# Cross-covariance attention and highway layer: stage 2 of a batch interleaved with the Gram sums of the next

## The chip, the cores and the metric

The kernel runs on one core of a Trainium2 chip. The metric is device time in microseconds, from the first to the last instruction of the core with what lies around it; lower is better. The time before is 414.52 us, the median of 3 runs (414.21 to 415.14).

TensorE (PE in the rows) multiplies 128x128 stationary tiles with moving tiles into PSUM; VectorE (DVE), ScalarE (ACT) and GpSimd (POOL) work on 128 partitions; SyncE (SP) only issues transfers here. Each engine runs its own instructions in order and waits on semaphores for the others.

## What is computed

There are four batches of 6336 rows and 256 channels. `tau` is 1.

```python
B, N, C = (4, 6336, 256)
qn = q / (np.linalg.norm(q, axis=1, keepdims=True) + 1e-06)
kn = k / (np.linalg.norm(k, axis=1, keepdims=True) + 1e-06)
s = kn.transpose(0, 2, 1) @ qn / tau
a = softmax of s over its last axis
x = (v @ a).reshape(B * N, C)
H = np.maximum(x @ w_h, 0.0)
T = 1.0 / (1.0 + np.exp(-(x @ w_t + b_t)))
out = T * H + (1.0 - T) * x
```

Inputs and output are fp32. The kernel loads q, k, v and the weights as fp16, and the transfer does the conversion. Read are 78 MB in all, written 26 MB.

## The kernel before

A sub-tile is 128 rows of one batch with all 256 channels; a batch has 49 full sub-tiles and a last one of 64 rows. Sub-tile s holds rows s·128 to s·128 + 127, one row a partition, so a partition reads runs of one row, 1 KB in HBM.

**Loads.** `_load_group` (L398) issues from POOL: one transfer for 16 sub-tiles (L401), and one for each sub-tile of the last group (L408). `load_qk` and `load_v` place these calls in the program. All q and k of a batch fit in their buffers (four each), v has three.

**Stage 1** (L120 to L149) runs over the 50 sub-tiles of a batch. For each half c of the channels it adds three products to `sg`: k by q (256 columns), k by k and q by q (128 columns each; their diagonals are the squared norms). That is 512 columns a half and six matmuls a sub-tile.

**The chain** (L151 to L248) makes of `sg` the matrix `mr`. ACT copies `sg` to `ssb`; DVE sums the diagonals (L162); ACT takes roots (L172, with a table load); DVE inverts them and spreads those of q into `dcat` (L178); TensorE broadcasts it (`cqb`); DVE scales (L193); ACT takes the exponential (L202, with a table load); DVE sums the rows, inverts and writes the softmax into the first 256 columns of `mr` (L210). TensorE transposes it and multiplies it by both weight matrices (`ahat`), which fills columns 256 to 767. So v has to be multiplied by `mr` only once.

**Stage 2** (L254 to L395) runs over pairs of sub-tiles, 24 full pairs and the last sub-tiles apart. `emit_transpose` transposes a pair of v with four matmuls by the identity into fp32 PSUM (`vtps`, L284), and DVE (L296) or ACT (L301), in turn, copies it to `vtsb` as fp16. It is called two pairs ahead. The pair is then multiplied by `mr`: columns 0 to 511 into `p3a` (x and H, one tile for each sub-tile, three buffers), columns 512 to 767 into `p3b`, to which a matmul with the identity adds the bias (L343). ACT makes `uu`, 1 − T (L354), and `hh`, the relu (L366). DVE makes `dd` = hh − x for each sub-tile (L370, 256 columns), POOL makes `pp` = uu·dd for the pair (L378, 512 columns), and DVE makes `o` = hh − pp (L382). SP stores eight sub-tiles at a time (L418).

**What sets the order.** The program is written batch after batch, stage 1, chain, stage 2. The framework's scheduler reorders it within its buffers, so that on TensorE some of the Gram sums of a batch stand between parts of stage 2 of the one before, and on DVE the steps of several pairs stand between each other. On each engine the result is one fixed row of instructions. A load on POOL takes the next of eight completion slots and waits until the load that had it last has landed.

## Time and profile before

| | before |
|---|---|
| median of the runs | 414.52 us |
| span of the profiled execution | 412.4 us |
| PE busy | 297.5 us (72%) |
| DVE busy | 208.9 us (51%) |
| ACT busy | 183.3 us (44%) |
| POOL busy | 189.2 us (46%) |
| DMA queue of POOL, share of 16 engines | 70.3% |
| DMA queue of SP, share of 16 engines | 20.6% |
| granted TensorE clock, mean | 0.950 of full speed |

The runs' time stands 2.1 us above the span of the profiled execution, which counts from the first to the last instruction. Busy time is counted per engine and overlaps between engines; a matmul's recorded length includes its way through the array, so that matmuls in a row start closer together than they last. The busy shares are means over stages with different limits, so the rows further below are mostly from single stretches.

### The profile page before, as it was taken

The numbers are of one execution on the slowest core, as the hardware profiler recorded it, in microseconds if no ns is written. First come the engines' busy times: TensorE is split into PE (matmuls) and PEld (weight loads), VectorE is DVE, ScalarE is ACT, GpSimd is POOL, SyncE is SP. The second block draws the span as 40 slices with busy tenths as digits, with TensorE's granted clock in tenths as the row PEclk, the third lists the DMA queues.
The fourth block names the chain that finished last, engine by engine and source line by source line (L and its number), as shares of the span: only waits on it lengthen the run. The fifth ranks groups of instructions, "written<-read, shape, count | busy, mean of one in ns | idle before, by whom it ended". The sixth has DMA issues, their size and how long they took to land.

```text
span 412.4 us, 6770 instructions
## 1 busy us (share of the span) xinstructions
PE 297.5 (72%) x2637; PEld 212.1 (51%) x2637; DVE 208.9 (51%) x426; ACT 183.3 (44%) x407; POOL 189.2 (46%) x173
## 2 busy tenths in 40 slices
PE   0186839809877899968777999777778938776770
PEld 0176737506544698544445986444447815444440
DVE  0000103707876704497767232887766144786663
ACT  1000126605655306756555055566552166655561
POOL 9212322634646634555548441557366002754453
PEclk9999969957999999999999999999999968999996
DMA  7999999999962999999439999494329700433333
GB/s 95 198 199 197 198 198 199 197 233 188 195 193 70 217 245 198 197 222 241 124 103 173 238 205 198 94 209 138 109 67 215 163 0 0 113 102 103 103 102 121
DMA packets 103456, 65.57 MB, mean 159 GB/s; under 512 B 1537, under 2 KB 103425, under 8 KB 103425
## 3 DMA queue, kind: packets, MB, share of 16 engines
q0 software_dynamic: 77568, 39.20, 70.3%
q1 hardware_dynamic: 25856, 25.95, 20.6%
q8 instruction: 20, 0.33, 0.3%
q14 instruction: 12, 0.09, 0.1%
HBM read 78.38 MB, written 25.95 MB: 253 GB/s over the span
## 4 chain that ended last, share of the span: by engine, by line
PE 24%; DMA 24%; DVE 23%; POOL 17%; issue 7%; ACT 4%; POOLq 0%; DVEq 0%; ACTq 0%
POOL pp L378 15%; DVE o L382 14%; DMA k<-in_k_dram 14%; DVE dd L370 7%; PE p3a L336 7%; DMA v<-in_v_dram 6%; PE sg L129 5%; DMA q<-in_q_dram 4%; PE p3b L329 3%; PE sg L136 2%; PE sg L143 2%; PE vtps L284 2%; ACT hh L366 2%; PE p3b L343 1%; DVE vtsb L296 1%
## 5 line engine op out<-in xcount | busy, mean ns | idle before, releaser
L378 POOL TENSOR_TENSOR pp<-uu,dd 128x512 f32<-128x512 f32 (+1 forms) x104 | 131.4, 1273 | 144.0 <-DVE dd L370 64.8
L336 PE MATMUL p3a<-mr,vtsb 128*128 128x512 f16 (+1 forms) x400 | 134.7, 385 | 33.6 <-DVE dd L370 33.5
L382 DVE TENSOR_TENSOR o<-hh,pp 128x512 f32<-128x512 f32 (+1 forms) x104 | 94.4, 923 | 52.3 <-POOL pp L378 52.3
L366 ACT ACTIVATE hh<-p3a 128x256 f32<-128x256 f32 x200 | 76.1, 386 | 87.1 <-PE p3a L336 57.5
L129 PE MATMUL sg<-q,k 128*128 128x256 f16 (+1 forms) x400 | 94.7, 281 | 25.0 <-DMA k<-in_k_dram 24.1
L329 PE MATMUL p3b<-mr,vtsb 128*128 128x256 f16 (+1 forms) x400 | 100.3, 276 | 0.6 <-ACT uu L354 0.5
L370 DVE TENSOR_TENSOR dd<-hh,p3a 128x256 f32<-128x256 f32 x200 | 75.4, 413 | 29.2 <-ACT hh L366 29.0
L136 PE MATMUL sg<-k 128*128 128x128 f16 (+1 forms) x400 | 89.8, 225 | 0.0
L143 PE MATMUL sg<-q 128*128 128x128 f16 (+1 forms) x400 | 89.7, 224 | 0.0
L296 DVE CAST vtsb<-vtps 128x512 f16<-128x512 f32 (+1 forms) x52 | 34.5, 664 | 98.4 <-PE vtps L284 98.1
L284 PE MATMUL vtps<-ident,v 128*128 128x128 f16 (+1 forms) x400 | 41.1, 222 | 34.9 <-DVE vtsb L296 22.7
L336 PEld LDWEIGHTS <-vtsb 128*128 128x128 f16 (+1 forms) x400 | 39.3, 99 | 42.4 <-issue 18.9
L329 PEld LDWEIGHTS <-vtsb 128*128 128x128 f16 (+1 forms) x400 | 39.3, 99 | 42.2 <-issue 26.7
L354 ACT ACTIVATE uu<-p3b 128x512 f32<-128x512 f32 (+1 forms) x104 | 59.8, 579 | 0.1
L284 PEld LDWEIGHTS <-v 128*128 128x128 f16 (+1 forms) x400 | 30.8, 99 | 54.2 <-issue 32.6
L129 PEld LDWEIGHTS <-k 128*128 128x128 f16 (+1 forms) x400 | 40.2, 100 | 30.5 <-DMA k<-in_k_dram 29.9
L343 PE MATMUL p3b<-btb,ident 128*128 128x256 f16 x200 | 55.2, 276 | 0.0
L143 PEld LDWEIGHTS <-q 128*128 128x128 f16 (+1 forms) x400 | 40.2, 101 | 6.9 <-issue 1.1
L301 ACT CAST vtsb<-vtps 128x512 f16<-128x512 f32 (+1 forms) x52 | 29.3, 563 | 29.2 <-PE vtps L284 29.2
L153 ACT COPY ssb<-sg 128x512 f32<-128x512 f32 x8 | 4.3, 589 | 84.7 <-PE sg L143 84.7
L136 PEld LDWEIGHTS <-k 128*128 128x128 f16 (+1 forms) x400 | 40.2, 101 | 1.7 <-issue 1.4
L401 POOL DMA_DIRECT2D k<-in_k_dram x12 | 14.1, 1176 | 27.9 <-PE sg L143 23.5
(44 smaller groups left out, 123.2 us busy)
## 6 DMA issues: line engine op xcount, KB each, us to landing
out_dram<-o SPq DMA_DIRECT2D x24, 1024.0 KB, 5.4
q<-in_q_dram POOLq DMA_DIRECT2D x12, 1024.0 KB, 19.6
k<-in_k_dram POOLq DMA_DIRECT2D x12, 1024.0 KB, 17.4
...
```

Of the source, the lines that this page charges most:

```text
L129: nc.tensor.matmul(sg[c][:, 0:C], kt_[0:nr, si, bass.ts(c, P)], qt[0:nr, si, :], start=first, stop=False,)
L136: nc.tensor.matmul(sg[c][:, C : C + P], kt_[0:nr, si, bass.ts(c, P)], kt_[0:nr, si, bass.ts(c, P)], start=False, stop=False,)
L143: nc.tensor.matmul(sg[c][:, C + P : C + 2 * P], qt[0:nr, si, bass.ts(c, P)], qt[0:nr, si, bass.ts(c, P)], start=False, stop=last,)
L284: nc.tensor.matmul(vtps[:, u, c, 0:nr], vt_in[0:nr, si + u, bass.ts(c, P)], ident[0:nr, 0:nr], start=(pcnt == 0), stop=(pcnt == 2 * pn - 1),)
L329: nc.tensor.matmul(p3b[0:nr, u, :], vt_sb[:, u, kt, 0:nr], mr[:, kt, 2 * C : 3 * C], start=(kt == 0 and u == 0), stop=False,)
L336: nc.tensor.matmul(pa[0:nr, :], vt_sb[:, u, kt, 0:nr], mr[:, kt, 0 : 2 * C], start=(kt == 0), stop=(kt == 1),)
L343: nc.tensor.matmul(p3b[0:nr, u, :], ident[:, 0:nr], btb, start=False, stop=(u == pn - 1),)
L354: nc.scalar.activation(out=uu[0:nr0, 0:pn, :], in_=p3b[0:nr0, 0:pn, :], func=Act.Sigmoid, scale=-1.0,)
L366: nc.scalar.activation(out=hh[0:nr, u, :], in_=p3a[u][0:nr, C : 2 * C], func=Act.Relu,)
L370: nc.vector.tensor_tensor(out=dd[0:nr, u, :], in0=hh[0:nr, u, :], in1=p3a[u][0:nr, 0:C], op=AluOp.subtract,)
L378: nc.gpsimd.tensor_tensor(out=pp[0:nr0, 0:pn, :], in0=uu[0:nr0, 0:pn, :], in1=dd[0:nr0, 0:pn, :], op=AluOp.mult,)
L382: nc.vector.tensor_tensor(out=ostg[0:nr0, si : si + pn, :], in0=hh[0:nr0, 0:pn, :], in1=pp[0:nr0, 0:pn, :], op=AluOp.subtract,)
```

## The change

The body of the kernel is written anew. What is computed stays; the two small constants of the reference are now added as well (1e-6 to the norms, 1e-9 to the sums).

**Layout.** Row p·49 + s of the first 6272 rows of a batch goes to partition p, so a chunk of 8 or 9 sub-tiles is one run of 8 or 9 KB per partition in HBM, for loads and stores. The last 64 rows of all four batches are loaded together, once for each of q, k and v (`tails`). q and k have nine buffers of a chunk each, v seven, the output three.

**Order.** The framework's scheduler is off (`manual_schedule`); what is written is what each engine runs. Stage 1 of batch 0 stands alone. Then in every pair of stage 2 TensorE gets: the pair's products, the transposes of the pair after next, and in pairs 0 to 17 a share of the 50 sub-tiles of the next batch's Gram sums. The five steps of the next batch's chain follow in pairs 18 to 22, one a pair. `issue_loads` places loads as soon as the buffer's last use stands earlier in the program.

**Steps.** Transposes are fp16 transposes into fp16 PSUM, all copied by DVE. `xh` takes the place of `p3a`, for a pair at once; the bias is one matmul of 512 columns a pair. `hh` and `dd` are one instruction a pair. The product is written over `dd`. `o` of a pair is written after the products of the next. The chain reads `sg` in PSUM, uses one scratch tile for the four diagonals, gets the row sums from the exponential, and multiplies in fp32 for the broadcast. PSUM: `sg` 2 banks, `xh` 2 × 2, `t` 1, `vt` 1.

```diff
-    GS = 16
-    OGS = 8
+NCH = [8, 8, 8, 8, 8, 9]
+QK_BUFS = 9
+V_BUFS = 7
+S1_SLOTS = 18
+LOOK = 2
...
+    ctx.enter_context(tc.manual_schedule())
...
+    def main_rows(src2d):
+        return src2d[0 : P * S, :].rearrange("(p s) c -> p s c", p=P)
+
+    def load_chunk(src, b, j, tag, bufs, store):
+        t = stream.tile([P, CM, C], f16, tag=tag, bufs=bufs, name=f"{tag}{b}_{j}")
+        n = NCH[j]
+        nc.gpsimd.dma_start(
+            out=t[:, 0:n, :], in_=main_rows(src[b])[:, c_start[j] : c_start[j] + n, :]
+        )
...
+    load_chunk(q, 0, 0, "q", QK_BUFS, q_t)
+    load_chunk(k, 0, 0, "k", QK_BUFS, k_t)
...
+        for j in range(NJ):
+            seq.append(("v", b, j))
+            if b + 1 < B:
+                seq.append(("q", b + 1, j))
+                seq.append(("k", b + 1, j))
...
+    def issue_loads():
+        while ptr[0] < len(seq):
+            kind, b, j = seq[ptr[0]]
+            bufs = V_BUFS if kind == "v" else QK_BUFS
+            prev = b * NJ + j - bufs
+            if prev >= 0:
+                at = done_use.get((kind, prev))
+                if at is None or at >= clock[0]:
+                    return
...
-                nc.vector.tensor_copy(
-                    out=vt_sb[:, 0:pn, :, 0 : nrows[0]],
-                    in_=vtps[:, 0:pn, :, 0 : nrows[0]],
-                )
-            else:
-                nc.scalar.copy(
...
+    def transposes(b, i):
+        ps = psum.tile([P, 2, 2, P], f16, tag="vt", bufs=1, name=f"vtps{b}_{i}")
+        for u, (src, nr) in enumerate(pair(b, i)):
+            for c in range(2):
+                nc.tensor.transpose(ps[:, u, c, 0:nr], src[:, bass.ts(c, P)], ident[0:nr, 0:nr])
...
+            nc.vector.tensor_copy(
+                out=vt[:, u0 : u0 + nu, :, 0:nr], in_=ps[:, u0 : u0 + nu, :, 0:nr]
+            )
...
+        xh = psum.tile([P, 2, 2 * C], f32, tag="xh", bufs=2, name=f"xh{b}_{i}")
+        tt = psum.tile([P, 2, C], f32, tag="t", bufs=1, name=f"t{b}_{i}")
...
+            nc.vector.tensor_tensor(
+                out=dd[0:nr, us, :],
+                in0=hh[0:nr, us, :],
+                in1=xh[0:nr, us, 0:C],
+                op=AluOp.subtract,
+            )
...
+            nc.gpsimd.tensor_tensor(
+                out=dd[0:nr, us, :], in0=uu[0:nr, us, :], in1=dd[0:nr, us, :], op=AluOp.mult
+            )
...
+    issue_loads()
+    for step in chain(0):
+        step()
+    for i in range(LOOK):
+        transposes(0, i)
...
+        for i in range(npair):
+            clock[0] += 1
+            xh, tt = main(b, i)
+            if pending is not None:
+                pending()
+            pending = elementwise(b, i, xh, tt)
+            n = i + LOOK
+            if n < npair:
+                transposes(b, n)
+            elif nxt:
+                transposes(b + 1, n - npair)
+            issue_loads()
+            if nxt:
+                want = min(S + 1, -(-(S + 1) * (i + 1) // S1_SLOTS))
+                while s1 < want:
+                    stage1(b + 1, s1)
+                    s1 += 1
+                if s1 == S + 1:
+                    if steps is None:
+                        steps = chain(b + 1)
+                    elif steps:
+                        steps.pop(0)()
```

Three places show how the rows of instructions change.

POOL, ahead of its first product of stage 2 in batch 0, before (the number in a tile's name is its place in the batch, `_460` and the like tell tiles apart; DMASW0 to DMASW7 are the completion slots):

```order
L401 DMA q_1_464<-in_q_dram 128x16x256 [waits DMASW0_49,PE_49]
L401 DMA k_1_465<-in_k_dram 128x16x256 [waits DMASW1_49]
L401 DMA q_2_468<-in_q_dram 128x16x256 [waits DMASW2_49,PE_49]
L401 DMA k_2_469<-in_k_dram 128x16x256 [waits DMASW3_49]
L408 DMA q_3_472<-in_q_dram 128x256 [waits DMASW4_49,PE_49]
L408 DMA q_3_472<-in_q_dram 64x256 [waits DMASW5_49]
L408 DMA k_3_473<-in_k_dram 128x256 [waits DMASW6_49]
L408 DMA k_3_473<-in_k_dram 64x256 [waits DMASW7_49]
L401 DMA v_0_478<-in_v_dram 128x16x256 [waits DMASW0_49]
L401 DMA v_1_480<-in_v_dram 128x16x256 [waits DMASW1_49]
L378 TENSOR_TENSOR pp_0_0_525<-uu_0_0_517,dd_0_0_520 128x512 [waits DVE_49,Activation_49]
```

Now the loads ahead of the first product end with the first chunks of v for batch 1 and of q and k for batch 2:

```order
L74 DMA v_4_442<-in_v_dram 128x2048 [waits DMASW7_49]
L74 DMA q_4_444<-in_q_dram 128x2048 [waits DMASW0_49,PE_49]
L74 DMA k_4_446<-in_k_dram 128x2048 [waits DMASW1_49]
L74 DMA v_5_448<-in_v_dram 128x2304 [waits DMASW2_49]
L74 DMA q_5_450<-in_q_dram 128x2304 [waits DMASW3_49,PE_49]
L74 DMA k_5_452<-in_k_dram 128x2304 [waits DMASW4_49]
L74 DMA v_0_454<-in_v_dram 128x2048 [waits DMASW5_49]
L74 DMA q_0_456<-in_q_dram 128x2048 [waits DMASW6_49,PE_49]
L74 DMA k_0_458<-in_k_dram 128x2048 [waits DMASW7_49]
L367 TENSOR_TENSOR dd_0_532<-uu_0_531,dd_0_532 128x512 [waits DVE_49,Activation_49]
L367 TENSOR_TENSOR dd_1_578<-uu_1_577,dd_1_578 128x512 [waits DVE_49,Activation_49]
```

What moved: where two chunks of v of the running batch and the rest of the next batch's q and k were last ahead of the product, more loads of a later use now are.

DVE in stage 2 of batch 1, before: the `dd` of two or three pairs, then their `o`.

```order
L370 TENSOR_TENSOR dd_0_8_1819<-hh_0_8_1818,p3a_8_1804 128x256
L370 TENSOR_TENSOR dd_0_8_1819<-hh_0_8_1818,p3a_9_1810 128x256
L370 TENSOR_TENSOR dd_0_10_1850<-hh_0_10_1849,p3a_10_1835 128x256
L296 CAST vtsb_1_0_1866<-vtps_1_0_1861 128x512
L370 TENSOR_TENSOR dd_0_10_1850<-hh_0_10_1849,p3a_11_1841 128x256
L370 TENSOR_TENSOR dd_0_12_1884<-hh_0_12_1883,p3a_12_1869 128x256
L370 TENSOR_TENSOR dd_0_12_1884<-hh_0_12_1883,p3a_13_1875 128x256
L382 TENSOR_TENSOR o_0_1657<-hh_0_8_1818,pp_0_8_1824 128x512
L382 TENSOR_TENSOR o_0_1657<-hh_0_10_1849,pp_0_10_1855 128x512
L382 TENSOR_TENSOR o_0_1657<-hh_0_12_1883,pp_0_12_1889 128x512
```

Now three instructions a pair, always in the same order (batch 0, pairs 2 and 3):

```order
L359 TENSOR_TENSOR dd_2_622<-hh_2_620,xh_2_608 128x512
L306 COPY vtsb_4_632<-vtps_4_627 128x512
L384 TENSOR_TENSOR o_0_574<-hh_2_620,dd_2_622 128x512
L359 TENSOR_TENSOR dd_3_672<-hh_3_670,xh_3_658 128x512
L306 COPY vtsb_5_682<-vtps_5_677 128x512
L384 TENSOR_TENSOR o_0_574<-hh_3_670,dd_3_672 128x512
```

The copy of the pair after next now stands between a pair's `dd` and its `o`, and `o` ahead of the next `dd`.

DVE at the chain, before (batch 1's chain, behind the last `o` of batch 0):

```order
L162 SCALAR_TENSOR_TENSOR junk_1591,nrm_1592<-ssb_1587,ident_70 128x128 x4
L296 CAST vtsb_0_4_1677<-vtps_0_4_1672 128x512
L174 RECIPROCAL inv_1599<-nrt_1597 128x4
L178 TENSOR_SCALAR dcat_1601<-ident_70,inv_1599 128x128 x2
L193 SCALAR_TENSOR_TENSOR t_1608<-ssb_1587,inv_1599,cqbs_1606 128x256 x2
L204 TENSOR_REDUCE rs_1613<-araw_1611 128x2
L208 RECIPROCAL rinv_1615<-rs_1613 128x2
L210 TENSOR_SCALAR mr_1590<-araw_1611,rinv_1615 128x256 x2
```

Now (batch 1's chain, in pairs 18 to 20 of batch 0):

```order
L306 COPY vtsb_20_1344<-vtps_20_1339 128x512
L181 SCALAR_TENSOR_TENSOR junk_1352,nrm_1353<-sg_544,ident_76 128x128 x4
L193 TENSOR_SCALAR inv_1360<-nrm_1358 128x4
L196 RECIPROCAL inv_1360<-inv_1360 128x4
L200 TENSOR_SCALAR dcat_1363<-ident_76,inv_1360 128x128 x2
L384 TENSOR_TENSOR o_4_1292<-hh_18_1332,dd_18_1334 128x512
L359 TENSOR_TENSOR dd_19_1380<-hh_19_1378,xh_19_1366 128x512
L306 COPY vtsb_21_1390<-vtps_21_1385 128x512
L384 TENSOR_TENSOR o_4_1292<-hh_19_1378,dd_19_1380 128x512
L359 TENSOR_TENSOR dd_20_1411<-hh_20_1409,xh_20_1396 128x512
L306 COPY vtsb_22_1421<-vtps_22_1416 128x512
L220 TENSOR_TENSOR t_1423<-sg_544,cqbs_1394 128x256 x2
```

The steps of the chain now stand between the copy of a pair and an `o`.

## Rows read from the trace of the kernel before

**Rows 1.** The head of the page.
```profile
span 412.4 us, 6770 instructions
```

**Rows 2.** Chain of waits in time order, first products of batches (start, length, what).
```profile
165.55 0.43 PE p3a L336 x2
...
252.51 0.43 PE p3a L336 x2
```

**Rows 3.** Busy time by stretch: length, PE, PEld, DVE, ACT, POOL, clock, DMA, GB/s.
```profile
168.00:223.00 55.00, 42.07 (x308) 26.36 (x306) 41.05 (x77) 34.11 (x82) 33.06 (x28) 1.00 0.90 173
```

**Rows 4.** Timeline of POOL: start, length, what, [idle before <- releaser].
```profile
3.74 1.21 POOL L401 DMA_DIRECT2D q<-in_q_dram  x1
...
67.78 1.15 POOL L401 DMA_DIRECT2D v<-in_v_dram  x1 [3.93 <-DMA k<-in_k_dram]
73.14 1.27 POOL L378 TENSOR_TENSOR pp<-uu,dd 128x512 f32<-128x512 f32 x1 [4.21 <-ACT uu L354]
```

**Rows 5.** DMA: 20 to 60 us, then by queue 137 to 153 us.
```profile
DMA packets 15584, 7.92 MB, mean 198 GB/s; under 512 B 176, under 2 KB 15582, under 8 KB 15582
...
q0 software_dynamic: 4473, 2.27, 104.0%
q1 hardware_dynamic: 1431, 1.40, 30.4%
```

**Rows 6.** Timeline of DVE in stage 2 of batch 2.
```profile
272.65 0.74 DVE L370 TENSOR_TENSOR dd<-hh,p3a 128x256 f32<-128x256 f32 x2
...
274.83 0.69 DVE L382 TENSOR_TENSOR o<-hh,pp 128x512 f32<-128x512 f32 x1 [0.84 <-POOL pp L378]
275.44 1.07 DVE L370 TENSOR_TENSOR dd<-hh,p3a 128x256 f32<-128x256 f32 x3
```

**Rows 7.** Timeline of POOL at the same place.
```profile
273.53 1.26 POOL L378 TENSOR_TENSOR pp<-uu,dd 128x512 f32<-128x512 f32 x1 [2.57 <-DVE dd L370]
276.26 1.26 POOL L378 TENSOR_TENSOR pp<-uu,dd 128x512 f32<-128x512 f32 x1 [1.47 <-DVE dd L370]
```

**Rows 8.** Timeline of PE in stage 1 of batch 1 and stage 2 of batch 2.
```profile
139.76 0.27 PE L129 MATMUL sg<-q,k 128*128 128x256 f16 x1
...
140.20 0.27 PE L129 MATMUL sg<-q,k 128*128 128x256 f16 x1
...
267.71 0.39 PE L284 MATMUL vtps<-ident,v 128*128 128x128 f16 x4
267.93 0.27 PE L329 MATMUL p3b<-mr,vtsb 128*128 128x256 f16 x1
...
269.45 0.39 PE L284 MATMUL vtps<-ident,v 128*128 128x128 f16 x4
```

**Rows 9.** Groups of instructions by line (xcount | busy us, mean ns | idle before).
```profile
L284 PE MATMUL vtps<-ident,v 128*128 128x128 f16 (+1 forms) x400 | 41.1, 222 | 34.9 <-DVE vtsb L296 22.7 <-DMA v<-in_v_dram 10.5 <-ACT vtsb L301 1.4
...
L172 ACT ACT_TABLE_LOAD x4 | 5.1, 1283 | 0.1
...
L162 DVE SCALAR_TENSOR_TENSOR junk<-ssb,ident 128x128 f32<-128x128 f32 x16 | 3.7, 285 | 0.0
L193 DVE SCALAR_TENSOR_TENSOR t<-ssb,inv,cqbs 128x256 f32<-128x256 f32 x8 | 3.5, 481 | 2.6 <-ACT cqbs L189 2.6
...
L210 DVE TENSOR_SCALAR mr<-araw,rinv 128x256 f16<-128x256 f32 x8 | 2.5, 351 | 0.1
...
L178 DVE TENSOR_SCALAR dcat<-ident,inv 128x128 f16<-128x128 f32 x8 | 1.9, 284 | 0.1
...
L174 DVE RECIPROCAL inv<-nrt 128x4 f32<-128x4 f32 x4 | 0.7, 178 | 10.5 <-ACT nrt L172 10.5
```

**Rows 10.** One line's or tile's instructions: ns min/median/max, first/last start; landings of stores.
```profile
L408 POOL DMA_DIRECT2D k<-in_k_dram x8: 528/561/590, 13.8 to 243.8; - x8
...
L378 POOL TENSOR_TENSOR pp<-uu,dd x104: 716/1267/1865, 73.1 to 407.2; 128x512 f32<-128x512 f32 x96, 128x256 f32<-128x256 f32 x4, 64x256 f32<-64x256 f32 x4
...
DMA to landing us min/median/max: 4.4/5.4/10.8
```

More of the change, by code (lines that the diff above doesn't have):

```diff
@@ new lines @@
+    ctx.enter_context(tc.manual_schedule())
+    q_t, k_t, v_t = {}, {}, {}
+    tails = {}
+    def main_rows(src2d):
[6 more added lines that the diff above has]
+        )
+        store[(b, j)] = t
@@ L74 @@
+    ones = const.tile([P, P], f32, tag="ones")
+    nc.vector.memset(ones, 1.0)
+    for j in range(1, 3):
+        load_chunk(q, 0, j, "q", QK_BUFS, q_t)
+        load_chunk(k, 0, j, "k", QK_BUFS, k_t)
+    wht = const.tile([P, 2, 2 * C], f16, tag="wht")
+    nc.gpsimd.dma_start(out=wht[:, :, 0:C], in_=moe_w_h.rearrange("(kt jl) m -> jl kt m", kt=2))
     nc.gpsimd.dma_start(
@@ new lines @@
+    for i in range(S + 1):
+        stage1(0, i)
+        clock[0] += 0.001
+    clock[0] += 1
[4 more added lines that the diff above has]
+        transposes(0, i)
+    pending = None
+    for b in range(B):
+        nxt = b + 1 < B
+        s1 = 0
+        steps = None
+        for i in range(npair):
+            clock[0] += 1
+            xh, tt = main(b, i)
[18 more added lines that the diff above has]
+                        steps.pop(0)()
+        while nxt and steps:
+            steps.pop(0)()
```

597 lines of the change are left out of this document (254 added, 343 removed).

## Prediction

> **What bounds the kernel now.** I read the stage windows first, then the chain of waits, then the timelines of POOL, DVE and PE. The chain of waits gives the rhythm: the first product of a batch on TensorE starts at 165.55 us in batch 1 and at 252.51 in batch 2 [rows 2], so a batch costs 87 us. Inside it no engine is full: in a stretch of stage 2, 55 us long, PE is busy 42, DVE 41, POOL 33 at a granted clock of 1.00 [rows 3]. What is late there is a loop through two engines. DVE subtracts (`dd`), POOL multiplies (`pp`), DVE subtracts again (`o`): `dd` starts at 272.65, `pp` at 273.53, `o` at 274.83, the next `dd` at 275.44, its `pp` at 276.26 [rows 6, 7]. Where the three follow each other like this, a pair of sub-tiles costs 2.7 to 2.8 us. TensorE needs less: at full clock a pair of stage 2 takes 269.45 − 267.71 = 1.74 us, and half a sub-tile of the Gram sums 0.22 us (two starts of L129, 0.44 us apart, hold both halves), so 0.44 us for a whole one [rows 8]. Per batch that is 25 × 1.74 + 50 × 0.44 = 65.5 us of PE.
>
> The front is bound by transfers. While only loads run, 198 GB/s of fp16 land, 396 GB/s as read in fp32 [rows 5]. POOL issues all loads, in program order, with eight completion slots: each issue waits until the load eight back has landed. At 67.78 POOL still waits for such a landing, and its first product of stage 2 is at 73.14 [rows 4].
>
> **1. The front.** All loads up to the last prefetch now stand on POOL ahead of the first product: 21 chunks of 8 or 9 sub-tiles stand there beyond batch 0's q and k, the tails and the weights. The last of them, `k_0_458`, waits for slot 7, that is for `v_4_442`. Read until then: q and k of batch 0 with 12.85 MB, weights and bias 0.79, three tails 0.79, five chunks of v 5.24, eight chunks of q and k of batch 1 8.39, together 28.05 MB; at 396 GB/s 70.8 us. The same count for before (24.0 MB by 67.78) leaves 7.2 us of start-up. q now goes first instead of at 3.74 [rows 4], so this is between 3.5 and 7.2; I take 4.8. Issuing the last load takes 0.56 us, the row of a load with one run per partition [rows 10]. The first product can start at 70.8 + 4.8 + 0.56 = 76 us. Batch 0's q and k land by 41 us (14.2 MB), and its Gram sums and some 10 us of softmax end by about 52: they hide under this, and DVE's first `o`, behind which TensorE soon waits too, stands until POOL comes.
>
> Runs per partition in HBM grow from 1 KB to 8 or 9 KB. No row shows such a load. For the slow end I take the store rate worked out in part 4 (311 GB/s; a rival of its own below), for the fast end as much the other way (480 GB/s: a front of 64 us); 396, the only load row, is the value.
> The Trainium skill, page "DMA: Bandwidth & Descriptors", section "Why small descriptors are slow (HBM only)", gives about 3 cycles of overhead per packet; estimated from it, with 32 cycles for 1 KB, the front would be 6 us shorter and the whole 370 us.
>
> **2. The pace of stage 2.** The new order on DVE is fixed: `dd` of a pair, the copy of a transposed pair, `o`, then the next `dd`. `o` waits for POOL's product, the product waits for `dd`, and the next `dd` stands behind `o`. The loop found above is thus closed for every pair, where before DVE often ran two pairs of `dd` ahead. Its length: `dd` on 512 columns in one piece 0.68 us (one piece of `o` with the same columns is 0.69 [rows 6]), hop to POOL 0.14 (0.74 us of two `dd` from 272.65, product at 273.53), product 1.26, hop 0.04, and 0.61 from the start of `o` to the next `dd` [rows 6, 7]: 2.73 us. The copy lies within the product and costs nothing while it ends before it (some 0.7 us, as `o` with the same columns, against 1.26); so its faster fp16 source, and that ACT has lost half of these copies, gain nothing here. Should POOL become shorter, the copy would be next.
>
> TensorE takes 1.74 us for stage 2 plus 50 sub-tiles over 18 pairs, 2.78 × 0.44 = 1.22: 2.96 us in pairs 0 to 17, and 1.74 in pairs 18 to 24. Against the loop this is 18 × 0.23 = 4.1 us too long, but PE enters each batch ahead, by what two buffers of `xh` allow; between 0 and 4.1, I take 1. Bias and product columns are the same as before.
>
> Pair 24 is in two pieces: 0.61 + 0.75 + 0.14 + 2 × 0.72 + 0.04 = 3.0 us (0.75 as two `dd` of 256 columns, shortest product 0.716 us [rows 10]).
>
> **3. The softmax chain between pairs 18 and 22.** Its steps are now in DVE's line. The norms: four reductions into one scratch tile, each waiting for the one before, 4 × 0.35 (0.285 and 0.07 for the hop); square root and hops 0.4; two short operations and two of 0.28, with hops 0.93 [rows 9]. Of these 2.7 us, 0.9 fit where DVE waited for POOL: 1.8. The softmax: two products 0.75, two exponentials 1.1 (estimated), two short ones and two of 0.35, overlapped, 1.1 [rows 9]: 2.95, less 0.9: 2.05. ACT changes its table four times a batch instead of three, 1.28 us each (one of three rows alike [rows 9]); two hide behind DVE, two hold up a sigmoid that POOL awaits by little. For these, the copy and the fold together 0.65. Sum 4.5 us; with no table load hidden 9.6, and at least 2, the reductions that fit no gap.
>
> **4. Loads in the loop.** Every fourth pair of batches 0 and 1 has three loads between two products: 3 × 0.56 = 1.68 us, where POOL has 0.61 + 0.68 + 0.14 + 0.04 = 1.47 to spare; some 0.24 a group, 1.4 a batch. In batch 2 a single load fits. The queue: in the window of 137 to 153 us, 2.27 MB landed in fp16 (4.54 read, 11.5 us at 396 GB/s) beside 1.40 MB stored [rows 5], so stores take 4.5 us for it, 311 GB/s. A group of three loads and one store needs 8.0 + 3.4 = 11.4 us against 4 × 2.73 + 0.24 = 11.2: level, with eight chunks in hand. I charge nothing.
>
> **Sum.** Batches 0 and 1: 24 × 2.73 + 3.0 + 4.5 + 1 + 1.4 = 75.4 each; batch 2: 74.0; batch 3, alone, from first product to last `o`: 24 × 2.73 + 1.44 + 0.04 + 0.75 = 67.7. The last store is of 1.18 MB, 5.4 us by the median landing of 1 MB [rows 10]. 76 + 75.4 + 75.4 + 74.0 + 67.7 + 5.4 = 373.9 us of span. The span before is 412.4 [rows 1], the median of the runs 414.5; with the same 2.1 us around it: **376 us**.
>
> **Rivals.**
> *The long runs are cut up again.* Then a load costs POOL what 2048 runs cost, 1.21 us [rows 4]: 3.63 a group, 1.9 more than charged, twelve groups: 376 + 23 = 399. For it: the page shows no load of this form. Against: loads with few runs take half. Chance 0.11.
> *Loads get slower, and the kernel slower than before.* Place: the front and the twelve groups, where the queue is level with the loop. At 300 GB/s the front grows by 23 us and each group to 10.5 + 3.4 = 13.9, 2.7 above the loop, twelve times 32: 431. It decides from about 325 GB/s (15 + 23 us). For it: 128 streams 49 KB apart, which no row tried. Against: fewer, longer runs ask no more of anything that the rows show. Chance 0.07.
> *Transposes in a row do not overlap.* One is recorded at 222 ns [rows 9], yet four start within 0.22 us, 0.055 apiece [rows 8]; with transposes of the other kind this overlap is unproved. At 0.222 each a pair with Gram sums takes 3.63 us, 0.90 above the loop: 18 × 0.90 less the 3.1 us of lead, three times, in place of 1: 376 + 36 = 412. Chance 0.05.
> The Trainium skill, "TensorE: Matmul & The Clock Gate", section "Part 4: PE-mode transpose", gives about 275 ns in one kernel's context and says that the mode does not count as busy for the clock; by 275 ns the estimate would be 424 us, slower than before. No row here shows that mode.
> *The clock falls to 1.2 GHz where PE waits for the loop.* The stretch of rows 3 had 1.00 at three quarters busy; batch 3 will have 1.74 of 2.73. At half the clock a pair takes 3.48 us: 24 × 0.75 = 18 us in batch 3, 16 more in pairs 18 to 24: 394 to 410. Chance 0.07.
>
> **How the numbers follow.** The forecast keeps 0.70, itself reaching from about 359 (fast front, cheap chain) to 392 (unhidden table loads, a waiting queue). With half of the first and last rivals, 358 to 400 leaves out some 2 in 10. A measurement tells 0.2% (0.8 us) from no change. Faster: 0.70 + 0.11 + 0.07 and most of the transposes, 0.91; within 0.2%: 0.02; slower: 0.07.
>
> **What would show it.** First product near 76 us with POOL waiting for a DMA; DVE starts of `o` 2.7 us apart in batch 3, released by POOL; four transposes within 0.25 us; single issues near 0.56 us; DVE's stops of about 2.7 and 3 us in pairs 18 and 20. Wrong if `o` waits for anything but POOL, if TensorE is released late by a load, or if the front ends far from 76.

## The result and the profile after

The changed kernel takes 380.01 us (median; 378.53 to 382.07), the kernel before, measured beside it, 414.56: a ratio of 0.917, with a 95% interval of 0.914 to 0.920. The forecast was 376 us. The profiled execution took 382.07 us with a span of 380.3, so 1.8 us lie around the span; the sum of the prediction stood at 373.9 for the span. The 6.4 us between are followed stage by stage below.

The front first. POOL's timeline at its end (start, length, engine, line, what, [idle before and what ended it]). POOL now writes its product over `dd`, so the product that was `pp` [rows 4, 7] reads `dd<-uu,dd`:

```profile
22.58 0.53 POOL L74 DMA_DIRECT2D q<-in_q_dram  x1 [1.28 <-DMA btb<-in_moe_b_t_dram]
24.72 0.53 POOL L74 DMA_DIRECT2D k<-in_k_dram  x1 [1.61 <-DMA btb<-in_moe_b_t_dram]
...
71.84 0.53 POOL L74 DMA_DIRECT2D q<-in_q_dram  x1 [2.17 <-DMA k<-in_k_dram]
74.05 0.53 POOL L74 DMA_DIRECT2D k<-in_k_dram  x1 [1.68 <-DMA v<-in_v_dram]
74.60 1.27 POOL L367 TENSOR_TENSOR dd<-uu,dd 128x512 f32<-128x512 f32 x1
```

The first product starts at 74.60, straight behind the last of the 21 prefetches, which waited for a chunk of v: 76 had been forecast, for this reason. In the same stretch the DMA view (26 to 66 us) shows 213 GB/s of fp16, that is 426 as read in fp32, where the 1 KB runs gave 198 and 396 [rows 5]; and an issue takes 0.53 us where it took 1.2 [rows 4]:

```profile
DMA packets 2534, 8.52 MB, mean 213 GB/s; under 512 B 267, under 2 KB 523, under 8 KB 2532
```

Now the stages. The table of windows has a row for each stretch between chosen products of POOL: length, busy us of PE, weight loads, DVE, ACT and POOL, granted clock, DMA share, GB/s. The rows are products 0 to 18 of batch 0, product 18 to the next batch's first, products 0 to 18 of batch 1, the same end stretch again, and the whole of batch 3:

```profile
74.60:127.94 53.34, 50.36 (x480) 37.88 (x480) 30.15 (x54) 19.29 (x33) 29.18 (x30) 0.94 1.05 250
127.94:152.41 24.47, 18.61 (x122) 10.52 (x121) 16.47 (x45) 15.40 (x27) 12.24 (x15) 0.93 0.79 181
152.41:204.43 52.02, 52.02 (x516) 39.46 (x515) 30.14 (x55) 21.69 (x37) 29.25 (x30) 1.00 1.03 233
204.43:229.21 24.78, 19.46 (x120) 10.86 (x119) 16.47 (x45) 15.39 (x27) 11.14 (x13) 0.86 0.72 160
...
305.78:373.30 67.52, 44.09 (x295) 24.73 (x294) 39.81 (x75) 27.97 (x49) 31.76 (x26) 0.99 0.23 95
```

Two limits take turns. In pairs 0 to 17 of batch 1 PE is busy 52.02 of 52.02 us: where Gram sums stand among the pairs, TensorE is the bound. In batch 3, which has none, it is busy 44 of 67.5 and the loop through DVE and POOL rules, to the hundredth as forecast. Two products there, and what the list of waits adds up for them (us in total, times, longest):

```profile
360.44 1.26 POOL L367 TENSOR_TENSOR dd<-uu,dd 128x512 f32<-128x512 f32 x1 [1.47 <-DVE dd L359]
363.18 1.27 POOL L367 TENSOR_TENSOR dd<-uu,dd 128x512 f32<-128x512 f32 x1 [1.47 <-DVE dd L359]
```
```profile
POOL dd L367 <- DVE dd L359: 114.3, 78, 1.8
DVE o L384 <- POOL dd L367: 113.8, 94, 14.1
...
POOL dd L367 <- ACT uu L354: 20.2, 7, 3.7
```

They start 2.74 us apart, and POOL idles 1.47 in between, as at the one place of the trace before that showed the loop [rows 7]. A run further down takes POOL out of the loop: batch 3 falls to 2.26 us a pair, while pairs 0 to 17 of batch 1 take 52.6 us there, no less than here.

Last, the softmax. The stretch from product 18 to the next batch is 24.1 to 24.8 us, where six pairs of 2.73 and one of 3.0 would be 19.4. In batch 2 POOL's timeline shows two of its three stops: the products are 4.12 and 4.51 us apart. ACT's timeline and, behind it, PE's at the same place show why:

```profile
281.65 1.27 POOL L367 TENSOR_TENSOR dd<-uu,dd 128x512 f32<-128x512 f32 x1 [1.57 <-DVE dd L359]
...
285.77 1.25 POOL L367 TENSOR_TENSOR dd<-uu,dd 128x512 f32<-128x512 f32 x1 [2.32 <-DVE vtsb L306]
290.28 1.27 POOL L367 TENSOR_TENSOR dd<-uu,dd 128x512 f32<-128x512 f32 x1 [3.26 <-ACT uu L354]
```
```profile
281.47 1.28 ACT L191 ACT_TABLE_LOAD   x1
283.08 0.20 ACT L191 ACTIVATE nrm<-nrm 128x4 f32<-128x4 f32 x1 [0.33 <-DVE junk L181]
283.19 0.58 ACT L351 ACTIVATE hh<-xh 128x512 f32<-128x512 f32 x1
283.79 1.28 ACT L354 ACT_TABLE_LOAD   x1
285.08 0.60 ACT L354 ACTIVATE uu<-t 128x512 f32<-128x512 f32 x1
```
```profile
285.73 0.79 PE L212 MATMUL cqb<-dcat,ones 128*128 128x256 f32 x2 [3.02 <-ACT uu L354]
286.32 1.91 PE L324 MATMUL xh<-mr,vtsb 128*128 128x512 f16 x4
```

ACT loads the table of the square root and then that of the sigmoid again, so the sigmoid of pair 19 ends at 285.68, and POOL's product follows at 285.77 (the profile names `vtsb`, which was long done). POOL's other operand was hardly earlier, for DVE had the four reductions, the wait for the root and the steps up to `dcat` to do first:

```profile
284.74 0.68 DVE L359 TENSOR_TENSOR dd<-hh,xh 128x512 f32<-128x512 f32 x1
```

It ends at 285.42; with the forecast's hop of 0.14 us the product could have started at about 285.56. So what this first stop, 4.12 us, has above 2.73 is mostly DVE's own steps and its wait for the root; the sigmoid adds some 0.2 us for POOL. It costs TensorE more. TensorE had stood still for 3.02 us by then: `cqb` shares the one buffer of `t` with the pairs, and that sigmoid empties it. Then TensorE ran at a granted clock of 0.62 (the window further down), so `xh` took 1.91 us and made pair 20 late. That is the second stop.

### The profile page after: what moved, and what is told of

Read it like the earlier page. It is cut to its first block, busy times and chain, and to the rows that moved or that the text cites. A ratio compares the mean times of both kernels' runs of the same rounds, so it can differ in the third digit from the quotient of the medians.

```text
span 380.3 us, 6361 instructions
## 1 busy us (share of the span) xinstructions
PE 294.3 (77%) x2540; PEld 204.1 (54%) x2540; DVE 186.9 (49%) x394; ACT 147.3 (39%) x251; POOL 170.7 (45%) x189
## 4 chain that ended last, share of the span: by engine, by line
PE 46%; DMA 17%; DVE 13%; POOL 12%; ACT 5%; issue 4%; POOLq 0%; DVEq 0%; ACTq 0%
PE xh L324 15%; POOL dd L367 11%; DMA k<-in_k_dram 9%; PE sg L160 8%; PE t L335 7%; DVE dd L359 6%; DVE o L384 5%; DMA v<-in_v_dram 5%; PE sg L162 4%; PE sg L161 4%; PE vtps L303 4%; PE t L331 3%; DMA q<-in_q_dram 3%; ACT L354 2%; ACT hh L351 2%
## 5 line engine op out<-in xcount | busy, mean ns | idle before, releaser
L367 POOL TENSOR_TENSOR dd<-uu,dd 128x512 f32<-128x512 f32 (+1 forms) x104 | 127.1, 1224 | 149.9 <-DVE dd L359 114.3
L384 DVE TENSOR_TENSOR o<-hh,dd 128x512 f32<-128x512 f32 (+1 forms) x100 | 70.1, 701 | 113.8 <-POOL dd L367 113.8
L160 PE MATMUL sg<-q,k 128*128 128x256 f16 x392 | 93.9, 281 | 19.8 <-DMA k<-in_k_dram 19.8
L324 PE MATMUL xh<-mr,vtsb 128*128 128x512 f16 (+1 forms) x400 | 108.0, 393 | 0.5 <-DVE vtsb L306 0.5
L161 PE MATMUL sg<-k 128*128 128x128 f16 x392 | 87.9, 224 | 0.0
L162 PE MATMUL sg<-q 128*128 128x128 f16 x392 | 87.8, 224 | 0.0
L359 DVE TENSOR_TENSOR dd<-hh,xh 128x512 f32<-128x512 f32 (+1 forms) x104 | 68.5, 662 | 12.3 <-ACT hh L351 11.2
L354 ACT ACTIVATE uu<-t 128x512 f32<-128x512 f32 (+1 forms) x104 | 59.9, 580 | 10.4 <-PE t L335 4.6
L335 PE MATMUL t<-mr,vtsb 128*128 128x256 f16 (+1 forms) x400 | 62.3, 279 | 0.0
L160 PEld LDWEIGHTS <-k 128*128 128x128 f16 x392 | 39.5, 101 | 20.3 <-DMA k<-in_k_dram 20.3
L161 PEld LDWEIGHTS <-k 128*128 128x128 f16 x392 | 39.5, 101 | 0.0
```

Of the source, the lines that this page charges most:

```text
L160: nc.tensor.matmul(sg[:, c, 0:C], ka[:, cs], qa, start=first, stop=False)
L161: nc.tensor.matmul(sg[:, c, C : C + P], ka[:, cs], ka[:, cs], start=False, stop=False)
L162: nc.tensor.matmul(sg[:, c, C + P : C + 2 * P], qa[:, cs], qa[:, cs], start=False, stop=last)
L324: nc.tensor.matmul(xh[0:nr, u, :], vt[:, u, kt, 0:nr], mr[:, kt, 0 : 2 * C], start=(kt == 0), stop=(kt == 1),)
L335: nc.tensor.matmul(tt[0:nr, u, :], vt[:, u, kt, 0:nr], mr[:, kt, 2 * C : 3 * C], start=False, stop=(kt == 1 and u == 0),)
L354: nc.scalar.activation(out=uu[0:nr, us, :], in_=tt[0:nr, us, :], func=Act.Sigmoid, scale=-1.0)
```

## The experiments

Each is the changed kernel with the edit shown. Times are medians; the changed kernel's 380.0 stands beside them. The kernel before, measured beside each, took 414.1 to 414.7. "Pair" is the distance of two products, and a batch's period that of two first products; where DVE makes the product, both are counted by `dd`.

### The loop: is it the order on DVE?

**The last subtraction one pair later.** The prediction explained the 2.73 us by the order on DVE: the next `dd` stands behind an `o` that waits for POOL.

```diff
...
-            if pending is not None:
-                pending()
-            pending = elementwise(b, i, xh, tt)
+            if len(pending) == 2:
+                pending.pop(0)()
+            pending.append(elementwise(b, i, xh, tt))
...
```

> The second subtraction `o` of a pair is issued one pair later on DVE, so that the next `dd` no longer stands behind a product that POOL has yet to make. Theory (the closed loop dd, product, o sets the pace wherever TensorE has no Gram sums): batch 3 falls from 2.73 us a pair to about 1.9, 24 x 0.8 = 20 us less; pairs 18 to 24 of batches 0 to 2 gain some 4 us each; pairs 0 to 17 gain nothing since TensorE's 2.96 us rule there: about 380 - 20 - 12 = 348 us (342 to 355). Rival (DVE and POOL slow each other so that their summed work is the bound, not their order): 372 us or more, batch 3 above 2.5 us a pair.

Measured: 372.25 us. Batch 3 runs at 2.56 us a pair, not 1.9; from its first product to its last `o` it is 5.2 us shorter, half of what the profiled execution gained. The wait of `o` is gone there, and its time has come back inside the instruction. First two products in POOL's timeline, then DVE's beside each:

```profile
303.36 1.92 POOL L367 TENSOR_TENSOR dd<-uu,dd 128x512 f32<-128x512 f32 x1 [1.35 <-DVE dd L359]
...
341.03 1.27 POOL L367 TENSOR_TENSOR dd<-uu,dd 128x512 f32<-128x512 f32 x1 [1.29 <-DVE dd L359]
```
```profile
303.48 0.67 DVE L384 TENSOR_TENSOR o<-hh,dd 128x512 f32<-128x512 f32 x1
304.08 0.67 DVE L359 TENSOR_TENSOR dd<-hh,xh 128x512 f32<-128x512 f32 x1
304.68 0.41 DVE L306 COPY vtsb<-vtps 128x512 f16<-128x512 f16 x1
...
341.14 1.70 DVE L384 TENSOR_TENSOR o<-hh,dd 128x512 f32<-128x512 f32 x1
```

At 341 the product has begun 0.11 us before the `o`. The product takes its usual 1.27, the `o` 1.70, ending 0.54 us after the product: nearly all of its work came after it. At 303 it is the other way round. The `o` takes 0.67, and the product, recorded from 303.36, takes 1.92, ending 1.13 after the `o`. Meanwhile `dd` and the copy, at 304.08 and 304.68, pass beside the product at their usual length; those two read PSUM, while `o` reads two operands in SBUF, as the product does. So one of the two holds the other off. Which one, the recorded starts don't tell: the product's is 0.11 or 0.12 us ahead in both places. Issuing `o` later does not take it out of the sum: the product and `o` add up all the same, and `dd`, which here too stands behind `o` on DVE, waits for both. An order with `dd` ahead of the late `o` was not run. There `dd` and the copy would pass beside the product, as at 304.08 and 304.68, and a pair would be an estimated 1.9 us, the product's 1.27 and 0.6 of `o`; so it is not shown that the order has no part.

The Trainium skill, page "SBUF — State Buffer", section "SBUF: two separate sides", says that DVE and GpSimd share a pair of SBUF ports as an exclusive lock, which a DVE instruction with two SBUF inputs takes too, against one of GpSimd that reads SBUF. The lines above agree: 1.70 instead of 0.67 us for `o`, and 1.92 instead of 1.27 for the product.

**The product on DVE.** If the two exclude each other, POOL's product is only a slow way to do work that DVE must stand aside for.

```diff
-            nc.gpsimd.tensor_tensor(
-                out=dd[0:nr, us, :], in0=uu[0:nr, us, :], in1=dd[0:nr, us, :], op=AluOp.mult
-            )
...
         def finish():
+            for u0, nu, nr in spans(b, i):
+                us = slice(u0, u0 + nu)
+                nc.vector.tensor_tensor(
+                    out=dd[0:nr, us, :], in0=uu[0:nr, us, :], in1=dd[0:nr, us, :], op=AluOp.mult
+                )
```

> The product `pp` goes from POOL to DVE, ahead of the `o` of its pair (one pair later than its `dd`); POOL only issues loads. In the run with the late `o` an `o` beside a product of POOL took 1.70 us, ending 0.54 us after that product, and 0.67 us alone. Theory (these two never work at the same time, so their times add up in any order: 1.26 + 0.61 + 0.60 + hops): with all four on DVE a pair costs 0.60 + 0.34 + 0.60 + 0.61 = 2.15 us, batch 3 some 14 us less, pairs 18 to 24 some 2 us less in each of three batches, the whole 359 us (354 to 364). Rival (the two run side by side and the late `o` was stretched by something else, so that POOL's 1.26 us carried work that DVE must now add): 2.5 us or more a pair in batch 3, the whole 374 us or more.

Measured: 354.14 us, a ratio of 0.858 (0.854 to 0.863) to the kernel before. DVE's timeline in batch 3:

```profile
300.43 0.68 DVE L368 TENSOR_TENSOR dd<-uu,dd 128x512 f32<-128x512 f32 x1
301.14 0.69 DVE L383 TENSOR_TENSOR o<-hh,dd 128x512 f32<-128x512 f32 x1
301.75 0.68 DVE L359 TENSOR_TENSOR dd<-hh,xh 128x512 f32<-128x512 f32 x1
302.35 0.42 DVE L306 COPY vtsb<-vtps 128x512 f16<-128x512 f16 x1
302.69 0.68 DVE L368 TENSOR_TENSOR dd<-uu,dd 128x512 f32<-128x512 f32 x1
```

One engine without a gap, 2.26 us a pair: all four operations on one engine take less than three of them, spread over two, took in a closed loop. By the starts of `dd`, batch 3 lost 11.6 us of 65.6, batches 1 and 2 lost 1.4 each, and batch 0 11.7, since the prefetches on POOL no longer hold a product up. That last part I had not counted, and of the 6 us that I had counted in pairs 18 to 24 at most 1.4 a batch came: the total, 5 us better than expected, agreed with the forecast better than its parts.

### The front: the queue of prefetches

**Nine loads first, then one a pair.**

```diff
-    def issue_loads():
-        while ptr[0] < len(seq):
+    def issue_loads(most):
+        upto = ptr[0] + most
+        while ptr[0] < min(upto, len(seq)):
...
-    issue_loads()
+    issue_loads(9)
...
-            issue_loads()
+            issue_loads(1)
```

> Nine loads instead of 21 ahead of the first product on POOL, then at most one a pair. Theory (POOL's in-order queue of loads holds back a first product whose operands have been ready since the first sigmoid ended at 62.4 us): first product at about 62.5 instead of 74.6 us, the whole about 368 us (365 to 371). Rival (the transfers themselves are the bound, so that later chunks come late and the gain is given back in batch 0): first product at 62.5, but batch 0 longer by 8 to 12 us, the whole 376 to 381.

Measured: 366.69 us; first product at 61.98, released by its sigmoid and no longer behind a load:

```profile
44.05 0.53 POOL L74 DMA_DIRECT2D k<-in_k_dram  x1 [1.94 <-DMA v<-in_v_dram]
61.98 1.27 POOL L368 TENSOR_TENSOR dd<-uu,dd 128x512 f32<-128x512 f32 x1 [17.40 <-ACT uu L355]
```

Batch 0's period grew by 0.6 us only: hardly anything is given back, so the theory holds. The deep prefetch ahead of the first pair cost 12.6 us; what many chunks in hand are worth later, this run does not single out. Batches 1 and 2 are 1.6 us shorter each, at the second stop of the softmax, by the clock (below). The prediction's "they hide under this" for the first softmax was right in the changed kernel, but with less room than it said: the first sigmoid ended at 62.4 us there.

**The bias as one row.** The two waits for `btb` above are for loads that spread one row over 128 partitions.

```diff
+    nc.vector.memset(btb, 0.0)
...
-        nc.gpsimd.dma_start(out=btb[:, u, :], in_=moe_b_t.partition_broadcast(P))
+        nc.gpsimd.dma_start(out=btb[0:1, u, :], in_=moe_b_t.partition_broadcast(1))
+    ones16 = const.tile([P, P], f16, tag="ones16")
+    nc.vector.memset(ones16, 1.0)
...
-        nc.tensor.matmul(tt, ident, btb, start=True, stop=False)
+        nc.tensor.matmul(tt, ones16, btb, start=True, stop=False)
```

> The bias is loaded into one partition (2 x 512 bytes) and spread by the product that adds it, with ones in place of the identity; the two loads that spread it to 128 partitions are gone. Theory (these two loads, 131 KB each, take some 2 us apiece in the queue): first product 3.5 to 4.5 us earlier, at about 70.5 us, the whole 375 to 377 us. Rival (those gaps are the queue's start and stay): first product at 74 to 75 us, the whole 379 to 381.

Rows 1 to 127 of `btb` are zero here. Measured: 376.54 us, first product at 71.56, that is 3.0 us earlier; the two waits are gone. The theory holds, with a little less than was expected.

### The parts of the change, one at a time

**Short runs again** (only the mapping of rows, in loads and stores).

```diff
-        return src2d[0 : P * S, :].rearrange("(p s) c -> p s c", p=P)
+        return src2d[0 : P * S, :].rearrange("(s p) c -> p s c", p=P)
```

> Only the mapping of rows to partitions is put back: runs of 1 KB per partition in HBM in loads and stores, the rest as changed. Theory (long runs give a front that reads at 428 instead of 396 GB/s and an issue of 0.55 instead of 1.2 us): front 5 us longer, each of twelve groups of three loads about 1.6 us longer: 380 + 5 + 20 = 400 to 407 us. Rival (only the rate of the transfers counts, POOL's longer issues lie in its idle time): about 386 us.

Measured: 389.5 us, nearer to the rival. The front is 5.5 us longer, as expected: the first product is at 80.07, and in the same stretch as above the DMA view shows

```profile
DMA packets 15646, 7.90 MB, mean 197 GB/s; under 512 B 252, under 2 KB 15645, under 8 KB 15645
```

197 against 213 GB/s, a factor of 1.08. The Trainium skill's 3 cycles of overhead per packet (page "DMA: Bandwidth & Descriptors", section "Why small descriptors are slow (HBM only)") would make it an estimated 35/32 = 1.09; the trace agrees. The issues, 0.9 us each, cost only 4.2 us over batches 0 and 1: a group of loads stretches one pair to some 3.9 us, and the next pairs fall to 2.73; TensorE's lead grows meanwhile (read from the pattern of the pairs, not tested by itself). The expectation had charged each group in full, as if no engine had a lead to spend.

**Transposes by ordinary products.** 

```diff
-        ps = psum.tile([P, 2, 2, P], f16, tag="vt", bufs=1)
+        ps = psum.tile([P, 2, 2, P], f32, tag="vt", bufs=1)
...
-                nc.tensor.transpose(ps[:, u, c, 0:nr], src[:, bass.ts(c, P)], ident[0:nr, 0:nr])
+                nc.tensor.matmul(
+                    ps[:, u, c, 0:nr], src[:, bass.ts(c, P)], ident[0:nr, 0:nr], start=True, stop=True
+                )
```

> The transposes of v as ordinary products with the identity into fp32, as before the change. Theory (the kind of transpose and the faster copy gain nothing, for the copy lies within POOL's product): copy 0.68 instead of 0.41 us, the whole 379 to 382 us. Rival (DVE's time counts): 0.27 us for each of 100 pairs, about 405 us; if only pairs paced by the loop count, some 52 pairs, 394.

Measured: 383.08 us (380.53 to 384.02), 1 us above the theory's range. The copy takes 0.66 instead of 0.40 us, and nearly all of it is hidden: batch 3 stays at 65.3 us from first product to last. Where DVE has the softmax too it shows: the first stop is 4.38 instead of 4.12 us in all three batches. So the new transposes bring at most some 3 us, of which the trace shows 0.8 at these stops, and not the rival's 14 to 25; the two kernels' runs overlap.

**No interleaving.**

```diff
-            if nxt:
+            if nxt and i == npair - 1:
                 want = min(S + 1, -(-(S + 1) * (i + 1) // S1_SLOTS))
```

> The Gram sums and the softmax of the next batch all stand behind pair 24 of the batch, not among its pairs. Theory (the interleaved order pays for the closed loop): each of three batches gains 22 us of TensorE and some 16 us of softmax and loses 9 to 13 us of TensorE's excess and of the stops: 380 + 3 x 26 = about 458 us (445 to 470), slower than the kernel before the change. Rival (TensorE's work comes out hidden either way by two buffers of xh): below 415 us.

Measured: 473.98 us, a ratio of 1.143 (1.140 to 1.145) to the kernel before. POOL's timeline at the end of batch 0:

```profile
140.39 1.40 POOL L367 TENSOR_TENSOR dd<-uu,dd 128x256 f32<-128x256 f32 x2 [1.20 <-DVE dd L359]
176.94 1.26 POOL L367 TENSOR_TENSOR dd<-uu,dd 128x512 f32<-128x512 f32 x1 [35.15 <-ACT uu L354]
...
188.49 0.53 POOL L74 DMA_DIRECT2D k<-in_k_dram  x1 [1.72 <-DMA v<-in_v_dram]
189.03 1.27 POOL L367 TENSOR_TENSOR dd<-uu,dd 128x512 f32<-128x512 f32 x1
```

For 35 us no product is made, as expected. What I missed, and what put the time 4 us above the range, stands behind it: eleven loads that could not be issued while q and k were in use now stand in front of the second product, so that the pair takes 12.1 us instead of 2.7. The interleaved order is what pays: in this form the gap of each batch is 36.6 to 36.9 us, where in the changed kernel the stops of the softmax cost about 5 and the Gram sums among the pairs 3 to 4.

### The stops at the softmax

**Without the square root** (the reciprocal is taken of the summed squares themselves).

```diff
-            nrm = small.tile([P, 4], f32, tag="nrm", name=f"nrm{b}")
-            nc.scalar.activation(out=nrm, in_=x, func=Act.Sqrt)
...
-                out=inv, in0=nrm, scalar1=1e-6, scalar2=None, op0=AluOp.add, op1=AluOp.bypass
+                out=inv, in0=x, scalar1=1e-6, scalar2=None, op0=AluOp.add, op1=AluOp.bypass
```

> The square root of the four norms is left out (the reciprocal is taken of the sums themselves), and with it two of ACT's four table loads a batch. Theory (the stop at pairs 18 and 19 is ACT's tables in front of a sigmoid that POOL awaits): 1.2 to 2.5 us less in each of batches 0 to 2, the whole 373 to 377 us; POOL waits for a sigmoid less than the 20.2 us of now. Rival (DVE's four reductions set that stop, as the prediction had it): 379 to 381 us.

Measured: 374.34 us. The line of waits, then two products of POOL in batch 2:

```profile
POOL dd L365 <- ACT uu L352: 8.7, 4, 2.8
```
```profile
281.39 1.26 POOL L365 TENSOR_TENSOR dd<-uu,dd 128x512 f32<-128x512 f32 x1 [1.88 <-ACT cqbs L212]
284.12 1.27 POOL L365 TENSOR_TENSOR dd<-uu,dd 128x512 f32<-128x512 f32 x1 [1.47 <-DVE dd L357]
```

8.7 us against 20.2. In batch 2 the three stops fall from 4.12, 4.51 and 4.80 to 3.69, 2.73 and 4.11: the second has vanished: TensorE stands still for 1.41 us at `cqb` instead of 3.02, and its clock stays at 1.00. So the square root and its two table loads are worth some 1.9 us a batch by the medians (by the profiled executions 1.2, 3.0 and 2.9 in batches 0 to 2). At the first stop only 0.43 us went. About 1 us remains there, and in it DVE runs without a gap, the four reductions and the steps up to `dcat` between two `dd`: so the rival is right for the first stop, and the theory for the second. In the third ACT still loads the table of the sigmoid between the exponentials and the sigmoid that POOL awaits (286.26 to 287.54, the product at 288.23).

**`cqb` in another buffer.**

```diff
-            cqb = psum.tile([P, C], f32, tag="t", bufs=1, name=f"cqb{b}")
+            cqb = psum.tile([P, C], f32, tag="vt", bufs=1, name=f"cqb{b}")
```

> The scale broadcast `cqb` of the softmax takes its PSUM from the tag of the transposes instead of that of `t`, so that TensorE no longer waits some 3.0 us for the sigmoid that empties `t` before it can go on to the `xh` of pair 20. Theory (this halt of TensorE, after which its granted clock was 0.50 and 0.62 in the pair, makes the second stop of a batch): product 19 to product 20 falls from 4.4, 5.0 and 4.5 us to about 3.0, the whole 375 to 377 us. Rival (ACT's table loads alone make it): 379 to 381 us.

Measured: 380.06 us, no change, as the rival had it. But it is no verdict on the halt, since the halt did not go: it only has another name. PE's timeline in batch 1:

```profile
208.97 0.70 PE L212 MATMUL cqb<-dcat,ones 128*128 128x256 f32 x2 [3.09 <-DVE vtsb L306]
```

TensorE now waits for the copy that empties the transposes' buffer, which stands on DVE behind the softmax's steps.

What that halt does differs from batch to batch, and the windows of pair 19 to pair 20 (columns as above) show with what it goes: batch 2 of the changed kernel, batch 2 with nine loads first, and batch 1 with the product on DVE (there from `dd` to `dd`).

```profile
285.77:290.28 4.51, 4.51 (x18) 2.40 (x19) 1.77 (x4) 1.62 (x4) 1.25 (x1) 0.62 0.82 252
```
```profile
272.15:275.24 3.09, 3.09 (x19) 1.86 (x20) 1.53 (x3) 1.76 (x4) 1.25 (x1) 1.00 0.72 168
```
```profile
197.21:199.76 2.55, 2.29 (x16) 1.51 (x17) 2.30 (x5) 1.18 (x3) 0.00 (x0) 1.00 1.05 213
```

Each time TensorE had stood still for 3.0 us at `cqb`, and each time the program gives it the same work. In the changed kernel the granted clock falls towards 0.5 (1.2 GHz) in all three batches and the pair takes 4.4 to 5.0 us; where it stays at 1.00 (2.4 GHz), in other runs, the pair takes 3.1 or less. So the rival "the clock falls" did come, in one pair of a batch and for 1.3 to 1.9 us. Why the same halt costs the clock in one batch and not in the other stays open.

**Gram sums over 20 pairs.**

```diff
-S1_SLOTS = 18
+S1_SLOTS = 20
```

> The Gram sums of the next batch are spread over 20 pairs instead of 18. Theory (TensorE's 2.96 us a pair rule pairs 0 to 17, its lead hides little): 2.84 us over 20 pairs, 20 x 0.11 = 2.2 instead of 18 x 0.23 = 4.1 us above the loop, some 1.9 less a batch, the whole 373 to 377 us. Rival (the lead hides the excess, and the softmax now ends too late for the next batch): 380 to 388 us.

Measured: 378.27 us (377.22 to 379.41): too close to 380.01 (378.53 to 382.07) to settle it. The periods of batches 0 and 1 fell by 0.7 and 0.2 us; batch 2's fell by 1.6, of which 1.4 is the clock at the second stop (3.09 instead of 4.51). And the last pair of batches 1 and 2 takes 3.5 instead of 2.8 us, for the softmax now ends late. The time lies between the two ranges, and neither theory is excluded.

### Put together

**Four edits at once**: the product on DVE, nine loads first, the bias as one row, `cqb` out of the buffer of `t`; each edit as above.

> Four edits together: the product on DVE, nine loads ahead of the first pair and then one a pair, the bias as one row, `cqb` out of the tag of `t`. By the runs so far, if each keeps its own: product on DVE 21 us (forecast), fewer loads first 13.3, bias 3.5, `cqb` 4 (forecast): 380 - 42 = 338 us (330 to 346). If TensorE's 2.96 us in pairs 0 to 17 and the softmax take back part of it: 345 to 352.

Measured: 356.57 us, outside both ranges and no better than the product on DVE alone (354.14). Nine loads first had nothing left to give, since no product stands behind the loads on POOL any more. The first `dd` came 2.7 us earlier, but batches 1 and 2 are 2.1 us longer each. In batch 1, pair 19 to 20 is

```profile
195.35:200.07 4.72, 3.65 (x13) 1.87 (x14) 2.30 (x6) 1.18 (x3) 0.00 (x0) 0.64 1.04 240
```

where the product on DVE alone had 2.55 us between two `dd` in batches 1 and 2. `cqb` waits 3.81 us there, for the copy, instead of 3.01; but the next run, without that edit, loses at the same place too, so what the buffer of `cqb` costs is not shown. The gains overlap; they don't add.

**The version kept**: the product on DVE and the bias as one row, both as above, and in batch 3 the copies on ACT:

```diff
...
-            nc.vector.tensor_copy(
-                out=vt[:, u0 : u0 + nu, :, 0:nr], in_=ps[:, u0 : u0 + nu, :, 0:nr]
-            )
+            if b == B - 1 and i >= LOOK:
+                nc.scalar.copy(
+                    out=vt[:, u0 : u0 + nu, :, 0:nr], in_=ps[:, u0 : u0 + nu, :, 0:nr]
+                )
+            else:
+                nc.vector.tensor_copy(
+                    out=vt[:, u0 : u0 + nu, :, 0:nr], in_=ps[:, u0 : u0 + nu, :, 0:nr]
+                )
...
```

> The product on DVE, the bias as one row, and in batch 3, which has no softmax beside it, the copy of the transposed pairs on ACT. Theory (what remains in batch 3 is DVE's own work: 2.26 us a pair with the copy, 0.34 of it the copy): bias 3 us, batch 3 at 1.90 to 1.95 us a pair, 23 x 0.33 = 7.5 us less: 354 - 3 - 7.5 = 343.5 us (341 to 347). Rival (ACT, then at 1.76 us a pair, delays `hh` and with it `dd`, so that batch 3 stays at 2.2 us): 350 to 353 us.

Measured: 348.21 us, a ratio of 0.840 (0.837 to 0.843) to the kernel before, the shortest of all. Batch 3 came down to 2.12 us a pair, not to 1.90. Two `dd` and the product between them on DVE:

```profile
298.90 0.68 DVE L367 TENSOR_TENSOR dd<-hh,xh 128x512 f32<-128x512 f32 x1
299.68 0.69 DVE L376 TENSOR_TENSOR dd<-uu,dd 128x512 f32<-128x512 f32 x1
300.41 0.69 DVE L391 TENSOR_TENSOR o<-hh,dd 128x512 f32<-128x512 f32 x1
301.02 0.68 DVE L367 TENSOR_TENSOR dd<-hh,xh 128x512 f32<-128x512 f32 x1
```

From `dd` to the product that reads it are now 0.78 us, where two operations in a row that don't depend on each other start 0.60 apart; the copy had filled that gap. So 0.14 of its 0.34 us a pair were gained, 3.1 us in batch 3 instead of 7.5. The profiled execution, 2.4 us above the median, shows the rest: batches 1 and 2 are 1.8 and 1.7 us longer than with the product on DVE alone, mainly at the second stop, 3.9 and 3.6 us at a granted clock of 0.50 and 0.59, where that run had 2.55 at 1.00. Against it, the front came 3.6 us earlier instead of 3.

## Why the prediction was right, and where it was not

*The front.* 76 us forecast, 74.60 measured, and released as forecast: POOL, its queue of loads, a landing of v. But two errors partly cancelled inside it. The rate was 426 instead of 396 GB/s, which by the short runs is 5.5 us; and the loads of the bias, whose bytes had been counted at that rate, took 3.0 us that were not in the sum.

*The pace of the loop.* 2.73 us forecast, 2.73 to 2.74 measured in all of batch 3, released by POOL; batch 3 with its last `o` 67.3 us against 67.7. The number was right because it was read from a place that showed the whole loop. Its explanation was half right: the forecast saw only the order on DVE, and the late `o` shows that the product and `o` do not run side by side, so that both stay in the sum when `o` is no longer waited for. That was not in the prediction.

*TensorE's lead.* This is the term that was mis-sized. Between 0 and 4.1 us a batch for the Gram sums in pairs 0 to 17, I took 1, and with 1.4 for loads in batches 0 and 1: 2.4, 2.4 and 1 above 18 pairs of 2.73. Measured are 53.3, 52.0 and 52.4 us against 49.1: 4.2, 2.9 and 3.3. The lead is used up after four to eight pairs, and then TensorE is the bound, at 3.06 us where a pair carries three Gram sub-tiles; the full 4.1 was nearer. The loads of batch 0, however, hide in those longer pairs, but for one group right at the start. (The charge for them was also added up too high: 1.68 − 1.47 is 0.21 us a group and 1.3 a batch.)

*The chain.* 4.5 us forecast, some 5 measured (three stops of 4.1, 4.4 to 5.0 and 4.8 to 5.0 us against 2.73, which is 5.2 in batch 0). The size came out right partly by luck. The two stops that were forecast came: the first, DVE's reductions and the square root, 1.4 us where 1.8 had been charged, and the third 2.1 to 2.3 where it was 2.05; of the 0.65 for the copy and the fold no stop shows. What was charged too much there offset part of what was missing, the second stop, 1.7 to 2.2 us. "two hold up a sigmoid that POOL awaits by little" was the step that failed: POOL does wait by little, but TensorE waits for the same sigmoid, 3.0 us, because `cqb` needs the buffer of `t`, and then runs at a granted clock of 0.50 to 0.62. Without the square root and its tables this stop is gone.

*The end.* 5.4 us after the last `o`, 7.2 measured: the last store of 1.18 MB landed 4.4 us after its issue, and some 3 us of span follow it.

*The sum.* In the span: front −1.4, batches 0 to 2 +2.4, +1.4 and +2.6, batch 3 −0.4, end +1.8, together +6.4. The median is another 2 us below the profiled execution, so 380 stands against 376.

*The rivals.* The long runs were not cut up: one issue is 0.53 to 0.60 us. Loads did not get slower but faster. Transposes overlap: the four of a pair start within 0.22 us, and the clock beside them is 0.99 in batch 3, with PE busy two thirds of the time:

```profile
355.22 0.38 PE L303 MATMUL vtps<-ident,v 128*128 128x128 f16 x4 [0.83 <-DVE vtsb L306]
355.44 1.03 PE L324 MATMUL xh<-mr,vtsb 128*128 128x512 f16 x4
```

The estimate of 424 us by the Trainium skill (page "TensorE: Matmul & The Clock Gate", section "Part 4: PE-mode transpose") needed 275 ns a transpose; the rows have 0.055 us apiece. The clock fell not where the prediction's rival had it, in batch 3 and pairs 18 to 24 throughout, but in single pairs after a halt.
